# A layer on one core: half of the normalized tiles transposed by DMA, the feed-forward weight loaded behind them, and a new schedule string

## The chip, the cores and the metric

The kernel runs on one core of a Trainium2 chip. The core has TensorE (PE in the profile; the loading of its stationary operand is listed as PEld), VectorE (DVE), ScalarE (ACT), GpSimd (POOL) and SyncE (SP), which here only issues DMAs. Matmuls read SBUF and write one of eight banks of PSUM; DVE and ACT read PSUM. The metric is the device time of one execution in microseconds; less is better.

## The reference

One transformer-like layer on 2048 tokens of width 640, in bf16. The input is normalized, and from the normalized input two branches are computed and summed with the input itself:

```python
xn = _layernorm(x)                      # (x - mean) / sqrt(var + 1e-5)
# attention: 32 query heads of 20, one head of K and V for all of them
q = (xn @ wq) -> [32 heads, 2048, 20];  k = xn @ wk;  v = xn @ wv
p = softmax(q k^T * 20 ** -0.5)         # 32 x 2048 x 2048
attn = concat_heads(p @ v) @ wo
# feed-forward, 640 -> 1728 -> 640
ffn = silu(xn @ w1) @ w2
out = x + attn + ffn
```

The large part is the score matrix: 32 heads times 2048 keys times 2048 queries, each exponentiated.

## The kernel before, in words

**Tiling.** The 2048 tokens are 16 tiles of 128. Queries are treated in four quarters of 512 (QC), heads in groups of four (HG), which gives 32 groups (NGR), each with 16 key tiles: 2048 score tiles of 128 keys by 512 queries. Four heads of width 20 lie on four strips of 32 partitions, so four score matmuls can use four row strips of PE at the same time (`s_mm`, recorded at line 1052). The value product of one key tile and four heads is four matmuls into four column strips (`pv_mms`, line 1175), accumulated in the PSUM bank UB, number 7. A further column of V gives the softmax's sum.

**Two ways to exponentiate.** ACT takes score tiles from two or three neighbouring banks and applies Exp in one instruction (line 1140), written to a ring Ebuf. DVE takes batches of four tiles, the four heads of one key tile: `dve_job` adds a bias and stores int16, whose bits read as bf16 are a power of two with a linear mantissa (line 1336). Two shifted copies of it (`dve_advance`, by POOL at line 1375 or by DVE at line 1380) correct the linear mantissa, and all three go through the value product. So a batch by DVE costs three groups of value matmuls, one by ACT costs one. The batch lies in one of the buffers `z_t`: three of their own and two in `zx`, and its copies in `s_t`.

**Prologue.** `pro_fill` orders the beginning in four blocks of four token tiles. `ln_pair` computes statistics on DVE (lines 550, 552, 554; for tiles 5 and 7 on ACT), the reciprocal root on POOL (line 559), and the normalized tile on DVE (first four, line 575) or POOL (line 572), into a ring `xn_ring` of XNR = 5 tiles. `tr_job` transposes a tile by five PE transposes of 128x128 (line 582) into a PSUM bank and copies it to `xnT` by ACT (first two, line 591) or DVE (line 594). Then `kT_job` makes K for four tiles (line 608; copied by ACT at line 618), `v_job` makes V (lines 632 and 640), and blocks 0 and 1 end with a chunk of Q (`q_job`; `QAT`). Q is scaled by DVE (line 679) and moved to the head strips by small DMAs (line 692).

**Feed-forward and output.** `h_job` makes one 128-wide chunk of the hidden layer: five matmul sets, tanh on ACT (line 756), product on DVE (line 759). `out_job` and, for the last quarter, `y_job` and `fin_job` multiply with w2 and wo in halves of 320 columns; `col_mm` (line 434) issues such a matmul as four column strips, `row_mm` (line 441) as row strips that can ride along with score matmuls. The 14th hidden chunk has only 64 real rows; for two quarters at a time it is made together (`h_pair`), rows 0 to 63 for the even quarter, 64 to 127 for the odd one, with zeros in the rest.

**What sets the order.** Nothing is ordered at run time. A planner in `build` runs through the work with assumed durations (`Sched`, `est`, `commit`) and writes down one order for each engine; `emit` adds the semaphore waits. Each engine then does its list in order. When several PE instructions are ready, `step_pe` picks by kind: scores for ACT ("s"), prologue ("m0"), score tiles for DVE ("d"), value products ("p", "pd"), other matmul jobs ("m", "l"). Its thresholds are in BASE, and every 10 us of planned time one letter of the string PLAN chooses a variation from RULES. In the prologue, score runs go alternately to banks 0 to 2 and 3 to 4 (ABUFS), other jobs to banks 5 and 6 (XBANKS), and DVE gets no score tiles (EARLY = 0). SP issues DMAs in order too, by the priority that `dma` is given; a DMA that must wait holds the ones behind it. The weight w1 (line 1435) has no wait before it and is issued between the first DMAs of Q; w2 (line 1438) and wo wait for the Q of group 1.

```python
dma("w1", lambda e: e.dma_start(w1_sb[:, :, :], wrow(B_w1)), D * F * 2, writes=[res("w1")], prio=1.0)
```

Of the kernel before, what the change touches and what calls it, by code (L numbers as in the profile page):

```python
# [37 lines left out]
XBANKS = (5, 6)  # L38
# [7 lines left out]
XNR = 5  # L46
# [35 lines left out]
EARLY = 0  # L82
# [14 lines left out]
BASE = dict(hold2=0, bnd=4, pj=6000.0, rows=0, rowmin=3, lagmax=6, lagp=0, lagj=6, openlag=5, late=-0.02, lead=0.01, leadmax=0.02, need=460.0, hold=300.0, dwant=600.0, slack=550.0, dnow=400.0, hungry=0.0, patience=0.0, keep=460.0, open=2, zcap=9, stay=0.0, homes=1, want=1, claim=6)  # L97
RULES = dict(a={}, b=dict(keep=0.0), c=dict(lagp=3), d=dict(lagp=5), e=dict(lagp=0), f=dict(patience=200.0), g=dict(dwant=0.0),
             h=dict(zcap=4), i=dict(zcap=3), j=dict(homes=0), k=dict(leadmax=-1.0, lead=-1.0), l=dict(lead=0.08, leadmax=0.1),
             m=dict(need=560.0), n=dict(hold=0.0), o=dict(stay=460.0), p=dict(open=1), q=dict(slack=400.0), r=dict(hungry=1000.0), s=dict(claim=9), t=dict(open=3), u=dict(claim=4), v=dict(want=2), w=dict(slack=700.0), x=dict(hold2=4), y=dict(bnd=0), z=dict(pj=-1e9), A=dict(rows=0), B=dict(rows=2, rowmin=2), C=dict(pj=2000.0), D=dict(openlag=3), E=dict(pj=8000.0), F=dict(hold2=3), G=dict(rows=1))  # L100
PLAN = "aaanGtxBBExhEhmxadrBBzraCBBEGqtrztfFzrqhwnpofocotyxddmGjvmpBaBitntqo"
# [17 lines left out]
class Op:  # L119
    __slots__ = ("eng", "fn", "occ", "lat", "pre", "reads", "writes", "prio", "mode", "slots",  # L120
                 "start", "fin", "done", "deps", "inc", "job", "first", "last", "gate", "on_commit", "seq", "name",
                 "dma_sem", "dma_val", "port", "run", "cut", "ends", "sync")

    def __init__(self, eng, fn, occ, lat=0.0, pre=(), reads=(), writes=(), prio=5.0, mode=None, slots=None,
# [24 lines left out]
        self.sync = None  # L149
        self.ends = (True, True)  # L150
# [52 lines left out]
class Sched:  # L203
# [71 lines left out]
    def commit(self, op, start):  # L275
# [20 lines left out]
        elif e == "sp":  # L296
            self.t[e] = start + op.occ
            own = 3300.0 if op.name == "dma wv" else 800.0 if op.name.startswith("dma pk") else 2000.0 if op.name.startswith("dma la") else 0.0
            self.dma_free = max(self.dma_free, start + 1300.0) + (op.lat - 800.0 if op.name.startswith("dma pk") else op.lat)
# [19 lines left out]
def build(nc, A_x, A_wq, A_wk, A_wv, A_wo, B_x, B_w1, B_w2, out, stack):  # L319
# [257 lines left out]

    def tr_job(n):
# [87 lines left out]
    def q_job(qc, k):  # L666
# [11 lines left out]
        xq_read[qc].append(job)  # L678
        op = Op("dve", lambda v: v.tensor_scalar_mul(q_st[:, st, :], bk(job.bank), QSCALE), t_dve(512), 140,  # L679
# [26 lines left out]
    xq_read = {k: [] for k in range(QC)}  # L706
    t_users = {}
    out_done = {}

    def h_pair(qb):  # L710
# [13 lines left out]
        for q in (qa, qb):  # L724
            xq_read[q].append(job.ops[-1])
        ts = (qb * FC + fk) % 2
# [16 lines left out]
    def h_job(qc, fk):  # L743
# [9 lines left out]
        xq_read[qc].append(job)  # L753
        ts = (qc * FC + fk) % 2
# [3 lines left out]
        extra = [norm_op[n] for n in range(NT)] + [o for n in range(NT) for o in tr_ops[n]] if par == 1 else [norm_op[n] for n in range(QTP + 6, QTP + 9)]  # L758
# [107 lines left out]
    def out_job(qc, i, hf):  # L866
        e0, e1 = hf * HALF, (hf + 1) * HALF
        mms = ffn_mms(qc, i, e0, e1, True, False) + o_mms(qc, i, e0, e1, False, True)
        job = pe_job(f"out{qc}_{i}_{hf}", mms, 19 * 140, gate=lambda: (qc, NG - 1) in pack_op, dyn=True)
        sl = (QTP * qc + i) % 3  # L870
# [18 lines left out]
    def y_job(qc, i, hf):  # L889
        e0, e1 = hf * HALF, (hf + 1) * HALF  # L890
        mms = ffn_mms(qc, i, e0, e1, True, not YC[i]) + o_mms(qc, i, e0, e1, False, True, range(YC[i]))
        job = pe_job(f"y{qc}_{i}_{hf}", mms, (14 + YC[i]) * 140, dyn=True)
        op = Op("dve", lambda v: v.scalar_tensor_tensor(out=yx[:, i, e0:e1], in0=bk(job.bank, 0, HALF), scalar=0.5,  # L893
# [114 lines left out]
    att = {"sgroup": 0, "pgroup": 0, "n": 0, "items": 0, "value": 0.0}  # L1008
# [49 lines left out]
    def plan(n):  # L1058

        if pro or n == 0:  # L1060
            buf = ABUFS[n % 2]
# [195 lines left out]

    def z_idle(k):
        b = z_last[k]
# [5 lines left out]
    def claim():  # L1265
        if z_slot() is None:
            return None
        g = att["sgroup"]
# [805 lines left out]
```

## Time and profile before

| | |
|---|---|
| median of three runs | 693.72 us (693.70 to 693.74) |
| profiled execution | 693.9 us |
| its span, first to last instruction | 692.1 us, TensorE clock 1.000 |
| busy PE / DVE / ACT / POOL | 680.5 / 572.0 / 673.5 / 593.0 us |
| score tiles by ACT | 655 instructions, 652.5 us busy |
| score tiles by DVE | 656 instructions, 428.8 us busy |
| moved by DMA | 28.97 MB |

The profile is one execution. Its views give the busy time of each engine over the span or a stretch of it; groups of equal instructions by source line, with their busy time, the mean of one and the idle time before them; the order of time; the chain of work that ended last; and DMA issues with the time until they landed. Lines are those of the kernel before; a helper's line stands for everything that calls it.

### The profile page before, as it was taken

The numbers are of one execution on the slowest core, as the hardware profiler recorded it, in microseconds if no ns is written. First come the engines' busy times: TensorE is split into PE (matmuls) and PEld (weight loads), VectorE is DVE, ScalarE is ACT, GpSimd is POOL, SyncE is SP. The second block draws the span as 40 slices with busy tenths as digits, with TensorE's granted clock in tenths as the row PEclk, the third lists the DMA queues.
The fourth block names the chain that finished last, engine by engine and source line by source line (L and its number), as shares of the span: only waits on it lengthen the run. The fifth ranks groups of instructions, "written<-read, shape, count | busy, mean of one in ns | idle before, by whom it ended". The sixth has DMA issues, their size and how long they took to land.

```text
span 692.1 us, 22655 instructions
## 1 busy us (share of the span) xinstructions
PE 680.5 (98%) x9908; PEld 229.7 (33%) x9911; DVE 572.0 (83%) x977; ACT 673.5 (97%) x727; POOL 593.0 (86%) x355
## 2 busy tenths in 40 slices
PE   8999999999999999999999999999999999999998
PEld 5432222222222333322223333322222333333344
DVE  7788889988988788789989878789898877888843
ACT  6899999999999999999999999999999999999993
POOL 6658999899988789898998879989889999988890
PEclk9999999999999999999999999999999999999999
DMA  8642220222221222233202222122222202232201
GB/s 223 194 158 39 20 22 14 35 33 27 22 19 14 37 39 24 29 74 35 27 9 28 31 29 33 22 63 41 30 20 21 22 19 31 31 68 23 23 7 40
DMA packets 34241, 28.97 MB, mean 42 GB/s; under 512 B 15486, under 2 KB 29662, under 8 KB 34142
## 3 DMA queue, kind: packets, MB, share of 16 engines
q1 hardware_dynamic: 33854, 27.20, 25.5%
q8 instruction: 77, 1.26, 0.7%
q10 hardware_dynamic: 288, 0.33, 0.1%
q14 instruction: 22, 0.18, 0.1%
HBM read 11.09 MB, written 2.62 MB: 20 GB/s over the span
## 4 chain that ended last, share of the span: by engine, by line
ACT 57%; PE 35%; DVE 5%; POOL 3%; issue 1%; DMA 0%
ACT sbt L1140 53%; PE psall L434 11%; PE psall L1175 11%; PE psall L1052 11%; ACT sbt L756 3%; POOL sbt L1375 2%; DVE sbt L1336 1%; DVE sbt L552 1%; DVE sbt L550 1%; DVE sbt L594 1%; POOL sbt L836 0%; DMA sbt<-in_A_x_dram 0%; PE psall L608 0%; PE psall L973 0%; DVE sbt L679 0%
## 5 line engine op out<-in xcount | busy, mean ns | idle before, releaser
L1140 ACT ACTIVATE sbt<-psall 128x1024 bf16<-128x1024 f32 (+1 forms) x655 | 652.5, 1220 | 2.2 <-PE psall L1052 1.7
L1375 POOL TENSOR_SCALAR sbt<-sbt 128x2048 int16<-128x2048 int16 x279 | 530.5, 1901 | 62.7 <-DVE sbt L1380 12.7
L1336 DVE TENSOR_SCALAR sbt<-psall 128x512 int16<-128x512 f32 x656 | 428.8, 684 | 79.6 <-PE psall L1052 72.0
L1052 PE MATMUL psall<-sbt 32*128 32x512 bf16 x2048 | 265.9, 384 | 3.7 <-ACT sbt L1140 1.8
L1175 PE MATMUL psall<-sbt 128*32 128x512 bf16 x3360 | 267.7, 384 | 1.2 <-DVE sbt L1223 0.4
L434 PE MATMUL psall<-sbt 128*32 128x320 bf16 (+2 forms) x3844 | 226.6, 331 | 0.7 <-ACT sbt L1140 0.5
L1052 PEld LDWEIGHTS psall<-sbt 32*128 32x128 bf16 x2048 | 70.0, 91 | 248.8 <-ACT sbt L1140 194.9
L434 PEld LDWEIGHTS psall<-sbt 128*32 128x32 bf16 x3844 | 83.9, 95 | 77.7 <-issue 46.9
L1175 PEld LDWEIGHTS psall<-sbt 128*32 128x32 bf16 x3360 | 66.0, 94 | 115.1 <-issue 82.4
L836 POOL TENSOR_TENSOR sbt<-sbt 128x512 bf16<-128x512 f32 x30 | 38.3, 1276 | 6.8 <-DVE sbt L1380 4.8
L759 DVE SCALAR_TENSOR_TENSOR sbt<-sbt,psall 128x512 bf16<-128x512 bf16 x52 | 35.5, 683 | 5.6 <-ACT sbt L756 4.9
L1380 DVE TENSOR_SCALAR sbt<-sbt 128x2048 int16<-128x2048 int16 x49 | 39.8, 827 | 0.2
L756 ACT ACTIVATE sbt<-psall 128x512 bf16<-128x512 f32 x52 | 39.5, 760 | 0.0
L1223 DVE COPY sbt<-psall 128x512 f32<-128x512 f32 x31 | 21.1, 682 | 2.3 <-PE psall L1175 2.2
L441 PE MATMUL psall<-sbt 32*128 32x320 bf16 (+1 forms) x60 | 20.5, 342 | 0.1
L1648 PE MATMUL psall<-sbt 128*32 128x256 bf16 (+1 forms) x264 | 18.1, 370 | 1.2 <-DVE sbt L474 1.2
L878 DVE SCALAR_TENSOR_TENSOR sbt<-psall,sbt 128x320 bf16<-128x320 f32 x24 | 11.6, 483 | 3.7 <-PE psall L434 2.6
L679 DVE TENSOR_SCALAR sbt<-psall 128x512 bf16<-128x512 f32 x20 | 13.5, 674 | 0.1
L893 DVE SCALAR_TENSOR_TENSOR sbt<-psall,sbt 128x320 f32<-128x320 f32 x8 | 3.9, 485 | 9.8 <-PE psall L434 9.7
L572 POOL TENSOR_SCALAR sbt<-sbt 128x640 bf16<-128x640 bf16 x12 | 10.4, 878 | 1.5 <-DVE sbt L564 1.2
L559 POOL TENSOR_TENSOR sbt<-sbt 128x2 f32<-128x2 f32 x8 | 5.6, 695 | 6.4 <-DVE sbt L557 6.1
L1648 PEld LDWEIGHTS psall<-sbt 128*32 128x32 bf16 x264 | 7.3, 113 | 6.2 <-issue 3.4
(63 smaller groups left out, 111.9 us busy)
## 6 DMA issues: line engine op xcount, KB each, us to landing
sbt<-sbt SPq DMA_DIRECT2D x120, 64.0 KB, 3.8
sbt<-in_A_x_dram SPq DMA_DIRECT2D x28, 160.0 KB, 3.3
sbt<-sbt SPq DMA_DIRECT2D x213, 20.0 KB
out_dram<-sbt SPq DMA_DIRECT2D x14, 160.0 KB, 1.9
sbt<-in_B_w_dram SPq DMA_DIRECT2D x1, 2160.0 KB, 12.7
sbt<-in_B_w_dram SPq DMA_DIRECT2D x1, 2080.0 KB, 8.2
sbt<-sbt SPq DMA_DIRECT2D x75, 8.0 KB
sbt<-in_A_wq_dram SPq DMA_DIRECT2D x1, 800.0 KB, 6.8
```

The costliest lines, as they stand in the source:

```text
L434: ins = pe.matmul(ps[j * SLOT:(j + 1) * SLOT, b * BANK + off:b * BANK + off + n], w[:, j * SLOT:(j + 1) * SLOT], x, start=start, stop=stop ...
L756: t = Op("act", lambda a: a.activation(t_buf[0:rows, ts, :], bk(job.bank, 0, QW, rows=rows), AF.Tanh, scale=0.5), t_act(512), 215, pre=[jo ...
L759: u = Op("dve", lambda v: v.scalar_tensor_tensor(out=hT[par][0:rows, fk, :], in0=t_buf[0:rows, ts, :], scalar=1.0, in1=bk(job.bank, 0, QW, ...
L836: nm = pool(lambda e: e.tensor_tensor(oU[:, us, :], U_sb[:, us, :], Rrep, ALU.mult), 1356.0, pre=[uc] + lc + pack_op.get(divmod(g - 2, NG) ...
L1052: return pe.matmul(bk(b), kT_rep[i * SLOT:(i + 1) * SLOT, kt * P:(kt + 1) * P], qT[i * SLOT:(i + 1) * SLOT, g % NQ, :], start=True, stop=T ...
L1140: return a.activation(Ebuf[:, es * QW:es * QW + w], ps[:, buf[0] * BANK:buf[0] * BANK + w], AF.Exp, scale=ESCALE)
L1175: ins = pe.matmul(ps[i * SLOT:(i + 1) * SLOT, UB * BANK:UB * BANK + QW], lhsT, rhs, start=(first and k < HG), stop=(last and k >= len(lst) ...
L1223: uc = Op("dve", lambda v: v.tensor_copy(U_sb[:, us, :], bk(UB)), t_dve(512), 140, pre=[pv] + up, reads=[sc.banks[UB]], writes=[res("U", u ...
L1336: p1 = Op("dve", lambda v: v.tensor_scalar(z16[:, i * QW:(i + 1) * QW], bk(job.bank), ZBIAS, 0.0, ALU.add, ALU.max), t_dve(QW) + 2.0, 140, ...
L1375: op = pool(lambda v, t=t, j=j, zin=zin: v.tensor_scalar(t.bitcast(I16), zin, float(SHIFT[j]), 1.0, ALU.add, ALU.mult), POOL_SHIFT, 0.0, p ...
L1380: op = dve(lambda v, t=t, j=j, zin=zin: v.tensor_scalar_add(t.bitcast(I16), zin, float(SHIFT[j])), t_dve(N, 4), prio=SPRIO - 0.01 * j, **args)
L1648: ins = pe.matmul(ps[i * SLOT:(i + 1) * SLOT, UB * BANK:UB * BANK + n], zero_t[:, 0:SLOT], zero_t[:, 0:n], start=fresh, stop=fresh, tile_p ...
```

## The change: what it does

- Tiles 8 to 15 (TRD = 8) are transposed by `tr_dma`: one transposing DMA from SP per tile, from `xn_ring` to `xnT`, with the highest priority on SP. The five PE transposes, the PSUM bank and the DVE copy go. The planner assumes 150 bytes per ns and 1300 ns more for it.
- `xn_ring` has eight tiles. All hidden chunks now wait for the whole prologue's normalization and transposes, since the ring lies partly in their buffer.
- w1 is issued only when the transposes of tiles 8 to 15 have landed.
- In the prologue, score runs are two banks each, on 0 and 1 or 2 and 3 (ARUN), and bank 4 is added to the other jobs' banks.
- DVE may take score tiles in the prologue (EARLY = 1) once tile 7 is normalized and the Q of group 1 is there; it then claims from the group behind ACT's.
- Three more batch buffers come from wq and w1 after their last reader (`Z_LENT`).
- The last hidden chunk is multiplied as the next to last, and in output jobs it may be issued as row strips, only the two that hold its 64 rows (`short`, `half`).
- The first jobs of the last quarter (`y_job`) may be made earlier.
- BASE has a pause before the next score run while ACT still has more than 520 ns of work (`stay`), two new thresholds (`pace`, `lagl`), and RULES and PLAN are new in part.

```diff
-XBANKS = (5, 6)
+XBANKS = (4, 5, 6)
+ARUN = ((0, 1), (2, 3))
-XNR = 5
+XNR = 8
+TRD = 8
+WTR = 4
+T_TR = 1300.0
+TR_RATE = 150.0
-EARLY = 0
+EARLY = 1
+EARLYN = 7
+EARLYG = 1
-BASE = dict(hold2=0, bnd=4, ..., zcap=9, stay=0.0, ...)
+BASE = dict(pace=-1.0, lagl=3, half=6, hold2=0, bnd=4, ..., zcap=9, stay=520.0, ...)
-PLAN = "aaanGtxBBExhEhmxadrBBzraCBBEGqtrztfFzrqhwnpofocotyxddmGjvmpBaBitntqo"
+PLAN = "aabgyzrzpFaxBGBrmJtxvEfyhdBwBrmxJaaawwdBhBKfiwkxkaaGxzGBmooBBtdttgtr"
...
+    NZ1 = len(z_t)
+    z_t.append(wq_sb[:, :, :].rearrange("p c d -> p (c d)")[:, 0:HG * QW])
+    z_t += [w1f[:, QTP * D + 2 * P + k * HG * QW:QTP * D + 2 * P + (k + 1) * HG * QW] for k in range(2)]
...
-    xn_ring = [h1f[:, (6 + i) * D:(7 + i) * D] for i in range(XNR)]
+    xn_ring = [h1f[:, (6 + i) * D:(7 + i) * D] for i in range(5)] + [h0f[:, (3 + i) * D:(4 + i) * D] for i in range(XNR - 5)]
...
+    def tr_dma(n):
+        xnT_op[n] = dma(f"tr{n}", lambda e: e.dma_start_transpose(xnT[:, :, n * P:(n + 1) * P], xn_ring[n % XNR]), P * D * 2,
+                        reads=[res("xn", n % XNR)], writes=[res("xnT", n)], pre=[norm_op[n]], prio=-1.0)
+        tr_ops[n] = [xnT_op[n]]
...
+    def short(job, qc):
+
+        for op in job.ops:
+            if hc_op[(qc, FC - 1)] in op.pre and op.cut is not None:
+                op.rows = tuple(range(HG))[:HG // 2] if qc % 2 == 0 else tuple(range(HG))[HG // 2:]
+        return job
...
-        for fk in range(FC):
+        for fk in [*range(FC - 2), FC - 1, FC - 2]:
...
-            buf = ABUFS[n % 2]
+            buf = ARUN[n % 2]
...
-        g = att["sgroup"]
+        g = att["sgroup"] + (1 if pro and EARLYG else 0)
...
             for n in range(4 * kc, 4 * kc + 4):
+                if n >= TRD:
+                    tr_dma(n)
+                    continue
                 j = tr_job(n)
...
+        d_w["w1"].pre += [tr_ops[n][0] for n in range(max(TRD, WTR), NT)]
...
-        if not pro or EARLY and 1 in q_op and all(o.done for o in q_op[1]) and len(xbanks()) >= EARLY:
+        if not pro or EARLY and (EARLYN not in norm_op or norm_op[EARLYN].done) and 1 in q_op and all(o.done for o in q_op[1]) and len(xbanks()) >= EARLY:
...
-        if not job.dyn or not ru.rows or sc.pe_mode != "s" or ...
+        if not job.dyn or not (ru.rows or ru.half) or sc.pe_mode != "s" or ...
+        if pick is None and not job.rest and len(piece.mms) > ru.half > 0:
+            x = next((x for x in list(piece.mms)[1:-1] if len(x.rows) < HG and all(p.done for p in x.pre)), None)
+            if x is not None:
+                pick = next(((x, r) for r in x.rows if r not in busy), None)
```

More of the change, by code (lines that the diff above doesn't have):

```diff
@@ L149, in __init__ @@
         self.sync = None
+        self.rows = tuple(range(HG))
         self.ends = (True, True)
@@ L1256, in build @@
     z_last = [None] * len(z_t)
+    lent_z = {}
+    Z_LENT = {NZ1: ("q", QC * DC), NZ1 + 1: ("h", QC * FC), NZ1 + 2: ("h", QC * FC)}
     def z_idle(k):
+        if k in Z_LENT and k not in lent_z:
+            w, n = Z_LENT[k]
+            if len(w_read[w]) < n or not all(o.done for o in w_read[w]):
+                return False
+            lent_z[k] = sc.order["pe"][-1]
         b = z_last[k]
@@ L1852, in commit_pe @@
                 cur_job[0].mms.remove(x)
-                job.rest[x] = list(range(HG))
+                job.rest[x] = list(x.rows)
             job.rest[x].remove(r)
```

31 lines of the change are left out of this document (19 added, 12 removed).

## The prediction

> **What bounds the kernel now.** I read the head of the page first, then the shares of the chain of waits, the busy time by stretches, the costliest groups with their shapes kept apart, the order of time around the edit, and the DMA issues.
>
> The head of the page and the chain's shares by engine:
>
> ```profile
> span 692.1 us, 22655 instructions
> PE 680.5 (98%) x9908; PEld 229.7 (33%) x9911; DVE 572.0 (83%) x977; ACT 673.5 (97%) x727; POOL 593.0 (86%) x355
> ...
> ACT 57%; PE 35%; DVE 5%; POOL 3%; issue 1%; DMA 0%
> ```
>
> Two engines are full at once, and the chain passes between them. Busy time by stretches (columns: stretch, its length, busy us and count of PE, PEld, DVE, ACT, POOL, then clock, DMA share, GB/s):
>
> ```profile
> 0.00:10.00 10.00, 8.26 (x157) 6.02 (x158) 6.39 (x21) 5.11 (x8) 7.00 (x22) 1.00 0.74 189
> 10.00:20.00 10.00, 9.44 (x135) 5.06 (x134) 9.64 (x35) 9.38 (x12) 6.31 (x8) 1.00 0.92 231
> 20.00:30.00 10.00, 9.59 (x128) 4.56 (x128) 8.72 (x33) 8.26 (x9) 7.27 (x10) 1.00 0.63 226
> 30.00:40.00 10.00, 9.66 (x121) 3.88 (x117) 5.11 (x12) 9.83 (x10) 1.52 (x3) 1.00 0.84 285
> 40.00:50.00 10.00, 9.87 (x133) 2.87 (x129) 9.14 (x15) 10.00 (x13) 7.65 (x5) 1.00 0.20 57
> ...
> 200.00:300.00 100.00, 99.14 (x1505) 32.52 (x1493) 81.75 (x134) 100.00 (x104) 86.56 (x49) 1.00 0.26 36
> ...
> 680.00:693.00 13.00, 8.79 (x238) 6.30 (x228) 5.14 (x10) 1.56 (x3) 0.00 (x0) 0.95 0.15 52
> ```
>
> From 40 us on ACT never rests, so a later gain can come only by taking exponentials away from ACT. The prologue loses 4.9 + 0.6 + 1.7 + 0.2 us of ACT in its first four stretches, and the tail 11.4 us. The change touches the second to fourth stretch and, through the rules, everything behind them; the first stretch and the tail stay.
>
> The groups of the shared work (last part: busy us, mean ns of one, idle before):
>
> ```profile
> L1375 POOL TENSOR_SCALAR sbt<-sbt 128x2048 int16<-128x2048 int16 x279 | 530.5, 1901 | 62.7 <-DVE sbt L1380 12.7 <-DVE sbt L1336 9.7 <-PE psall L1175 8.0
> L1336 DVE TENSOR_SCALAR sbt<-psall 128x512 int16<-128x512 f32 x656 | 428.8, 684 | 79.6 <-PE psall L1052 72.0 <-PE psall L441 3.0
> ...
> L1140 ACT ACTIVATE sbt<-psall 128x1024 bf16<-128x1024 f32 x573 | 555.0, 1172 | 0.3
> L1140 ACT ACTIVATE sbt<-psall 128x1536 bf16<-128x1536 f32 x82 | 124.6, 1555 | 1.9 <-PE psall L1052 1.7
> ```
>
> A score tile is 128x512. ACT exponentiates 573 x 2 + 82 x 3 = 1392 of them, DVE 656, together 2048. The page has both ACT forms together at 652.5 us:
>
> ```profile
> L1140 ACT ACTIVATE sbt<-psall 128x1024 bf16<-128x1024 f32 (+1 forms) x655 | 652.5, 1220 | 2.2 <-PE psall L1052 1.7
> ```
>
> So a tile costs ACT 652.5 / 1392 = 0.469 us, and a batch of four that DVE takes over saves ACT 1.88 us. What it costs PE is read from the order of time on PE:
>
> ```profile
> 60.81 0.39 PE L1052 MATMUL psall<-sbt 32*128 32x512 bf16 x4
> 61.13 0.62 PE L434 MATMUL psall<-sbt 128*32 128x512 bf16 x8
> 61.68 0.39 PE L1052 MATMUL psall<-sbt 32*128 32x512 bf16 x2
> 62.00 1.06 PE L1175 MATMUL psall<-sbt 128*32 128x512 bf16 x16
> 62.99 0.39 PE L1052 MATMUL psall<-sbt 32*128 32x512 bf16 x4
> 63.32 0.40 PE L1175 MATMUL psall<-sbt 128*32 128x512 bf16 x4
> ```
>
> A score set holds PE 0.32 us (60.81 to 61.13) whether two or four tiles ride in it. Two value groups of four matmuls hold it 0.55 us, four hold it 0.99, so one more is 0.22. A batch by DVE needs three value groups where ACT's needs one: +0.44 us of PE.
>
> **The change part by part.** *Eight tiles leave PE and DVE.* Between 21 and 37 us stand exactly the groups that go:
>
> ```profile
> L594 DVE COPY sbt<-psall 128x640 bf16<-128x640 bf16 x8 | 3.7, 485 | 1.4 <-PE psall L582 1.4
> ...
> L582 PE MATMUL psall<-sbt 128*128 128x128 bf16 x40 | 3.6, 221 | 0.0
> ```
>
> This removes 3.6 us of PE and 3.7 us of DVE, and eight uses of a PSUM bank. Bounds for PE: 0, if its time is filled by waits, and 3.6; I take 3.6, since PE was busy over nine tenths there.
>
> The Trainium skill ("TensorE: Matmul & The Clock Gate", Part 4: PE-mode transpose) gives about 275 ns for one 128x128 transpose inside a kernel, which as an estimate would make 40 of them 11 us. The trace disagrees: 40 take 3.6 us here, because they are pipelined, and the sum goes by that.
>
> *Eight DMAs come onto SP's queue.* Order of time around them (start, length, engine, line):
>
> ```profile
> 16.30 1.41 SPq L1435 DMA_DIRECT2D sbt<-in_B_w_dram  x1
> ...
> 24.39 5.11 SPq L692 DMA_DIRECT2D sbt<-sbt  x7
> ...
> 29.25 1.74 POOL L572 TENSOR_SCALAR sbt<-sbt 128x640 bf16<-128x640 bf16 x2 [0.30 <-DVE sbt L564]
> ...
> 30.73 0.39 SPq L1438 DMA_DIRECT2D sbt<-in_B_w_dram  x1
> ...
> 32.22 0.89 DVE L594 COPY sbt<-psall 128x640 bf16<-128x640 bf16 x2 [0.68 <-PE psall L582]
> ...
> 35.88 0.64 ACT L618 ACTIVATE sbt<-psall 128x512 bf16<-128x512 f32 x1
> ...
> 37.14 2.05 DVE L1336 TENSOR_SCALAR sbt<-psall 128x512 int16<-128x512 f32 x3 [0.61 <-PE psall L1052]
> ...
> 49.33 0.73 ACT L756 ACTIVATE sbt<-psall 128x512 bf16<-128x512 f32 x1
> ```
>
> Now the last two tiles are normalized by 30.99 and transposed by 33.11, 2.1 us later; K for tiles 12 to 15 is copied at 35.88, about when ACT has used up the first twelve. No row shows a transposing DMA. The nearest are these (KB each, us from issue to landing):
>
> ```profile
> sbt<-sbt SPq DMA_DIRECT2D x120, 64.0 KB, 3.8
> sbt<-in_A_x_dram SPq DMA_DIRECT2D x28, 160.0 KB, 3.3
> ...
> sbt<-in_B_w_dram SPq DMA_DIRECT2D x1, 2160.0 KB, 12.7
> sbt<-in_B_w_dram SPq DMA_DIRECT2D x1, 2080.0 KB, 8.2
> ```
>
> Bounds: 3.3 us, the load of as many bytes, and 9.5 us, the 64 KB row's rate on 160 KB. I take 3.8: a move within SBUF. The planner allows 4.4 (1.3 + 163,840 / 150 = 1.1, + 0.7 + 1.3), so nothing ordered behind them should stall. The last tile is then 1.7 us later behind its normalization (3.8 against 2.1). Against that, the four copies of tiles 8 to 11 no longer stand before the last statistics on DVE, 4 x 0.485 = 1.9 us, and eight buffers in place of five let POOL run ahead. Taken at nothing; if the cover fails it costs those 1.7 us of ACT once. SP's own issuing: seven pieces of Q took 5.1 us, 0.73 each; eight more are 5.8 us in a stretch from 17.75 to 33 where SP was not full. What waits in that queue is the second half of those Q pieces, and group 1 behind them: 2 to 3 us later, but no longer behind the 2160 KB weight.
>
> *The weight goes behind them.* From issue at 16.30 to some 35; it lands between 43 and 48, by the two weight rows. Its first use shows at 49.33. Cover: 1 to 6 us. With the second weight issued ahead of it, 8.2 us more, it would be late by up to 7; then feed-forward jobs slip behind attention work that is ready, and nothing is lost but order. Nothing taken; bound +2.
>
> *Score runs of two and two banks in the prologue, a third spare bank.* Between 12.8 and 37 us ACT ran 18 exponentials, alternately three and two tiles, 45 tiles in 20.9 us, which is 0.464 a tile:
>
> ```profile
> L1140 ACT ACTIVATE sbt<-psall 128x1536 bf16<-128x1536 f32 (+1 forms) x18 | 20.9, 1249 | 1.5 <-PE psall L1052 1.5
> ```
>
> The whole span's mean, nearly all two-tile, is 0.469: 45 x 0.005 = 0.2 us. Taken +0.2.
>
> *DVE starts on scores before the prologue ends.* It now begins at 37.14. It needs group 1's Q pieces (24.39 + 5.11 = 29.50, and 30.73 landed), so it can start near 31: some six us, eight tiles, two batches. This is where the shift below finds room on DVE. More than five batches can't be ahead (five buffers until a weight is done with), and 13 tiles are done by 48 us already (DVE's score tiles alone, by stretches):
>
> ```profile
> 37.00:48.00 11.00, 8.48 (x13) 1.00 0.45 154
> ```
>
> *Short last feed-forward chunk.* 32 output jobs have a chunk with only 64 real rows; two row groups of it may ride in score sets. One 320-wide chunk holds PE 0.66 / 4 = 0.165 us with its share of the switch:
>
> ```profile
> 654.97 0.73 PE L434 MATMUL psall<-sbt 128*32 128x320 bf16 x16
> 655.63 0.82 PE L1052 MATMUL psall<-sbt 32*128 32x512 bf16 x4
> ```
>
> All would save 32 x 0.14 (without the switch) = 4.4 us, none 0. Sets of four leave no row free, sets of two leave two; I take half, 2.2 us.
>
> *The rest* (later buffers in used-up weights, the order of chunks, earlier last-quarter jobs, the pause before scores, the string): order only. It could win or lose; a switch saved is 0.32 - 0.22 = 0.1 us, so a tenth of 655 score runs is 6.5 us either way. Taken at nothing.
>
> *The sum.* PE has 3.6 + 2.2 = 5.8 us to spare, ACT none. Moving x batches to DVE brings them level: 5.8 - 0.44 x = 1.88 x, x = 2.5, and both end 4.7 us sooner. DVE and POOL have the room: 2.5 batches are 10 tiles of 428.8 / 656 = 0.65, or 6.5 us of DVE, and five shifts of 1.9, against 79.6 and 62.7 us of waiting and the 3.7 removed. Half of the ACT gaps between 20 and 30 us go too, 0.9, as the transposes and bank uses between score runs go. Less 0.2: together -5.4. The profiled execution took 693.9 us (692.1 and 1.8 around it), so 688.5 for it; against the median of 693.72, 0.2 lower, 688.3.
>
> **The rivals.** *The transposes land late (slower).* Order is fixed when the program is built; each us beyond the allowed 4.4 delays K for tiles 12 to 15, and ACT takes key tiles in order, so it idles. For it: 9.5 us by the slowest row. Landing at 9.5 costs 5.1 and with the gain kept ends level; if, besides, they pass one at a time at 2.5 us a tile, the eighth is 8 x 2.5 = 20 us after the first at about 20, at 40 and not 35, and with the 9.5 us at its end it is some 10 us late: 688.3 + 10 = 698. It decides from 5.4 us late. Against it: loads of the same size land in 3.3.
>
> The Trainium skill ("VectorE: DVE Perf Modes", The three transpose paths) speaks for it: 1309 ns for a 128x128 block by DMA, and TensorE preferred. As an estimate, five blocks a tile one after another are 6.5 us, and eight tiles 52 us. The same skill ("DMA: Bandwidth & Descriptors", Latency and other measured facts) gives 261 GB/s for transposing DMAs, which is an estimate of 0.63 us a tile and no delay. No run here shows either yet.
>
> *The new order starves ACT (slower).* A pause before scores that is too long leaves ACT without tiles: 1% of the 640 us at 100% is 6.4 us, 694.7 with the gain kept. Against it: PE's waits for ACT are many and ACT's for PE few.
>
> *The freed time is not taken up (no change).* PE fills it with waits, ACT keeps 1392 tiles: only the gap time, 0.9 less 0.2: 693.0.
>
> *More than balance (faster).* All short chunks ride along (4.4) and a tenth of the switches is saved (half of 6.5): PE has 3.6 + 4.4 + 3.2 = 11.2 spare, x = 4.8, -9.1 and the gaps: 684.
>
> **How the numbers follow.** Forecast 0.47 (its own range 686 to 691.5), more than balance 0.22, not taken up 0.11, order starving ACT 0.10, late transposes 0.10. Predicted 688.3. Within 0.2% (1.4 us, about what a measurement of this kernel tells from no change) lie most of "not taken up" and a little of the slower two: 0.09; faster 0.73; slower 0.18. For 8 in 10: 683 leaves out part of the fast case, 696 the worst of the late one.
>
> **What would show it.** Right: no PE transposes and DVE copies after about 21 us; DMA transposes landing in 3 to 5 us; the first DVE score tile near 31; ACT over 9.5 in 20 to 30; DVE tiles up from 656 to about 666. Wrong: K's matmuls for tiles 8 to 15 waiting for a DMA, an ACT gap of microseconds at 30 to 40, or ACT below 99% after 50. The prediction falls if DVE's count stays while ACT's gaps stay.

## The result, and the profile after

The changed kernel takes 706.64 us (median of four, 705.34 to 707.81) against 693.71 us (693.62 to 693.74) for the kernel before, measured beside it. The ratio is 1.0182 with a 95% interval of 1.0169 to 1.0195: slower by 12.9 us, where 5.4 us less were forecast. The profiled execution took 705.34 us, 1.3 below the median.

The head of the page and the chain's shares by engine, of the changed kernel:

```profile
span 703.4 us, 22552 instructions
PE 683.2 (97%) x9846; PEld 226.8 (32%) x9849; DVE 569.1 (81%) x962; ACT 673.9 (96%) x733; POOL 605.0 (86%) x362
...
ACT 77%; PE 16%; DVE 3%; DMA 1%; SPq 1%; POOL 1%; issue 0%; POOLq 0%
```

ACT has as much work as before, 673.9 us against 673.5, in a span that is 11.3 us longer: it waits more. The groups of the shared work say that the split is the old one:

```profile
L1169 ACT ACTIVATE sbt<-psall 128x1024 bf16<-128x1024 f32 (+1 forms) x661 | 654.2, 1243 | 7.3 <-PE psall L1081 7.2
...
L1373 DVE TENSOR_SCALAR sbt<-psall 128x512 int16<-128x512 f32 x656 | 432.4, 686 | 96.5 <-PE psall L1081 89.8 <-PE psall L452 3.0
```

DVE has 656 score tiles in both kernels: no batch moved. Busy time by stretches (columns as in the prediction) shows where ACT waits:

```profile
10.00:20.00 10.00, 9.20 (x126) 4.95 (x124) 9.82 (x35) 8.81 (x14) 5.64 (x8) 1.00 0.87 234
20.00:30.00 10.00, 9.84 (x125) 3.34 (x125) 7.40 (x27) 9.43 (x11) 8.67 (x11) 1.00 0.53 81
30.00:40.00 10.00, 6.21 (x72) 2.09 (x71) 0.54 (x3) 6.31 (x7) 0.73 (x2) 0.79 0.34 70
40.00:50.00 10.00, 9.69 (x105) 2.85 (x109) 5.76 (x12) 6.49 (x7) 1.46 (x1) 0.70 0.89 311
50.00:60.00 10.00, 9.63 (x96) 2.33 (x93) 8.21 (x14) 8.93 (x11) 8.33 (x6) 0.83 0.68 249
60.00:100.00 40.00, 38.86 (x500) 11.58 (x492) 35.70 (x59) 39.76 (x47) 32.94 (x19) 1.00 0.24 29
200.00:300.00 100.00, 99.19 (x1535) 33.78 (x1536) 79.70 (x127) 100.00 (x106) 93.77 (x52) 1.00 0.26 34
...
690.00:704.00 14.00, 10.12 (x280) 7.46 (x272) 5.61 (x11) 0.00 (x0) 0.00 (x0) 1.00 0.14 49
```

Between 30 and 60 us ACT misses (is idle for) 3.7 + 3.5 + 1.1 = 8.3 us, where it missed 0.2 before. Later it is full again, and behind its last exponential PE still has 10 us of matmuls. The order of time on SP, and then the instructions on PE and DVE that waited (the bracket is the idle time before them and who ended it):

```profile
20.79 6.01 SPq L590 DMA_TRANSPOSE sbt<-sbt  x4
26.85 1.53 SPq L709 DMA_DIRECT2D sbt<-sbt  x2
28.43 2.53 SPq L590 DMA_TRANSPOSE sbt<-sbt  x2
31.00 1.49 SPq L709 DMA_DIRECT2D sbt<-sbt  x2
32.54 2.53 SPq L590 DMA_TRANSPOSE sbt<-sbt  x2
35.11 2.11 SPq L709 DMA_DIRECT2D sbt<-sbt  x3
40.28 0.41 SPq L1478 DMA_DIRECT2D sbt<-in_B_w_dram  x1
...
36.92 1.06 PE L624 MATMUL psall<-sbt 128*128 128x512 bf16 x2 [2.07 <-DMA sbt<-sbt]
40.31 0.60 PE L1081 MATMUL psall<-sbt 32*128 32x512 bf16 x2 [1.78 <-DMA sbt<-sbt]
...
40.95 1.29 DVE L1373 TENSOR_SCALAR sbt<-psall 128x512 int16<-128x512 f32 x2 [9.52 <-PE psall L1081]
```

The answer for the transposing DMAs alone:

```profile
L590 SPq DMA_TRANSPOSE sbt<-sbt x8: 1200/1268/1832, 20.8 to 33.8; - x8
...
DMA to landing us min/median/max: 2.6/2.7/3.7
```

They land in 2.7 us, sooner than the 3.8 forecast. But each holds SP's queue for 1.27 us (median), not the 0.73 of a piece of Q: the eight take 6.01 + 2.53 + 2.53 = 11.1 us of it, of which some 0.3 us are a wait for GpSimd, and the last piece of group 1's Q leaves at 37.2 us, against 29.5 before. From 20.8 to 37.2 us SP has no other pause. Two instructions on PE wait for what this queue issues. The K matmuls for tiles 12 to 15 wait 2.07 us for the last transposes. In the middle of the same K job the order has a score set of group 1 for DVE, which waits for all of Q's pieces until 40.31; some 1.8 us of that are a late landing of the last pieces, which the last section comes back to. PE does its list in order, so ACT's scores behind those two come late: that is the first stall. What SP has queued behind it is late too, down to the moment when GpSimd normalizes group 0, that is, multiplies its value product by the reciprocals of the softmax sums, which come to it by DMAs from SP. First in the changed kernel, then in the kernel before:

```profile
79.47 1.28 POOL L863 TENSOR_TENSOR sbt<-sbt 128x512 bf16<-128x512 f32 x1 [0.79 <-DMA sbt<-sbt]
```

```profile
65.03 1.27 POOL L836 TENSOR_TENSOR sbt<-sbt 128x512 bf16<-128x512 f32 x1 [0.66 <-DVE sbt L1380]
```

### The profile page after: what moved, and what is told of

The parts are those of the page before. It is cut to its first block, busy times and chain, and to the rows that moved or that the text cites. A ratio compares the mean times of both kernels' runs of the same rounds, so it can differ in the third digit from the quotient of the medians.

```text
span 703.4 us, 22552 instructions
## 1 busy us (share of the span) xinstructions
PE 683.2 (97%) x9846; PEld 226.8 (32%) x9849; DVE 569.1 (81%) x962; ACT 673.9 (96%) x733; POOL 605.0 (86%) x362
## 4 chain that ended last, share of the span: by engine, by line
ACT 77%; PE 16%; DVE 3%; DMA 1%; SPq 1%; POOL 1%; issue 0%; POOLq 0%
ACT sbt L1169 73%; PE psall L1204 5%; PE psall L445 5%; PE psall L1081 5%; ACT sbt L776 3%; DMA sbt<-sbt 1%; DVE sbt L561 1%; DVE sbt L563 1%; SPq L590 0%; DMA sbt<-in_A_x_dram 0%; SPq L709 0%; DVE sbt L568 0%; POOL sbt L570 0%; PE psall L1002 0%; POOL sbt L1412 0%; DVE sbt L1373 0%
## 5 line engine op out<-in xcount | busy, mean ns | idle before, releaser
L1412 POOL TENSOR_SCALAR sbt<-sbt 128x2048 int16<-128x2048 int16 x286 | 542.6, 1897 | 60.9 <-DVE sbt L1417 17.2
L1081 PE MATMUL psall<-sbt 32*128 32x512 bf16 x2048 | 269.4, 387 | 8.7 <-ACT sbt L1169 4.8
L445 PE MATMUL psall<-sbt 128*32 128x320 bf16 (+3 forms) x3728 | 227.5, 333 | 1.0 <-ACT sbt L1169 0.4
L1081 PEld LDWEIGHTS psall<-sbt 32*128 32x128 bf16 x2048 | 71.1, 91 | 257.9 <-ACT sbt L1169 190.9
L445 PEld LDWEIGHTS psall<-sbt 128*32 128x32 bf16 (+1 forms) x3728 | 80.1, 96 | 79.1 <-issue 49.7
L1204 PEld LDWEIGHTS psall<-sbt 128*32 128x32 bf16 x3360 | 67.9, 94 | 116.0 <-issue 79.4
L452 PE MATMUL psall<-sbt 32*128 32x320 bf16 (+1 forms) x122 | 39.4, 323 | 0.0
L1417 DVE TENSOR_SCALAR sbt<-sbt 128x2048 int16<-128x2048 int16 x42 | 35.7, 864 | 0.1
L1689 PE MATMUL psall<-sbt 128*32 128x256 bf16 (+1 forms) x296 | 20.2, 362 | 1.2 <-DVE sbt L485 1.2
L452 PEld LDWEIGHTS psall<-sbt 32*128 32x128 bf16 x122 | 11.1, 91 | 0.9 <-PE psall L445 0.7
L1689 PEld LDWEIGHTS psall<-sbt 128*32 128x32 bf16 x296 | 8.2, 109 | 7.3 <-issue 4.3
```

The costliest lines, as they stand in the source:

```text
L445: ins = pe.matmul(ps[j * SLOT:(j + 1) * SLOT, b * BANK + off:b * BANK + off + n], w[:, j * SLOT:(j + 1) * SLOT], x, start=start, stop=stop ...
L452: return pe.matmul(ps[0:w.shape[-1], b * BANK:b * BANK + n], w[k], x[k], start=start, stop=stop, tile_position=(r * SLOT, 0))
L1081: return pe.matmul(bk(b), kT_rep[i * SLOT:(i + 1) * SLOT, kt * P:(kt + 1) * P], qT[i * SLOT:(i + 1) * SLOT, g % NQ, :], start=True, stop=T ...
L1204: ins = pe.matmul(ps[i * SLOT:(i + 1) * SLOT, UB * BANK:UB * BANK + QW], lhsT, rhs, start=(first and k < HG), stop=(last and k >= len(lst) ...
L1412: op = pool(lambda v, t=t, j=j, zin=zin: v.tensor_scalar(t.bitcast(I16), zin, float(SHIFT[j]), 1.0, ALU.add, ALU.mult), POOL_SHIFT, 0.0, p ...
L1417: op = dve(lambda v, t=t, j=j, zin=zin: v.tensor_scalar_add(t.bitcast(I16), zin, float(SHIFT[j])), t_dve(N, 4), prio=SPRIO - 0.01 * j, **args)
```

## The experiments

A string of rules belongs to the kernel for which it was chosen: a new plan would change all of the order at once. So in each run below the order was planned as it stands, and one thing was edited in it afterwards. The kernel before took 693.97 or 693.98 us beside the first eight, 694.32 beside the last four. Diffs show what matters; left-out lines are marked.

**Plain copies in the transposes' place.** The transposition itself is left out.

```diff
-        xnT_op[n] = dma(f"tr{n}", lambda e: e.dma_start_transpose(xnT[:, :, n * P:(n + 1) * P], xn_ring[n % XNR]), P * D * 2,
+        xnT_op[n] = dma(f"tr{n}", lambda e: e.dma_start(xnT[:, :, n * P:(n + 1) * P], xn_ring[n % XNR].rearrange("p (c t) -> p c t", c=DC)), P * D * 2,
```

> The order of the changed kernel on every engine, with the eight transposing DMAs replaced by plain copies of the same 160 KB into the same place (so xnT holds untransposed tiles 8 to 15: the transposing is left out). A plain issue held SyncE 0.73 us where a transposing one held it 1.27. Theory A, the issue time on SyncE's queue is what delays the last Q pieces and K for tiles 12 to 15: 8 x 0.54 = 4.3 us less in front of them, the last Q piece lands near 35 instead of 40.3, ACT's idle time between 30 and 60 us falls from 8.3 us to 2 or less, the clock stays at 1.00, and the time is 697 to 699 us. Rival B, the waiting is for the data and not for the queue, or the loss is in the new order behind 60 us: 704 to 707 as now.

Measured: 702.0 us, ratio 1.0121 (1.0097 to 1.0145). Only 4.6 us came back, where 7.6 to 9.6 were expected. The first stall is gone, by this kernel's stretches, but a later one stands in its place:

```profile
30.00:40.00 10.00, 9.60 (x137) 3.58 (x135) 3.23 (x10) 9.16 (x11) 0.62 (x2) 1.00 0.58 177
40.00:60.00 20.00, 19.64 (x237) 5.52 (x233) 19.22 (x32) 20.00 (x23) 15.25 (x9) 1.00 0.61 219
60.00:80.00 20.00, 16.96 (x199) 4.96 (x198) 15.18 (x26) 17.23 (x20) 14.77 (x9) 0.96 0.31 32
```

```profile
73.78 1.26 POOL L863 TENSOR_TENSOR sbt<-sbt 128x512 bf16<-128x512 f32 x1 [3.42 <-DMA sbt<-sbt]
```

ACT misses 2.8 us between 60 and 80. GpSimd waits 3.42 us for group 0's sums, whose DMAs stand in SP's queue behind the loads of wo, of its end, of w2 and 22 pieces of Q; the shift for DVE's next batch stands behind it on GpSimd. So there are two stalls in a row, and taking away the first uncovers the second.

**Plain copies that hold the queue as long as the transposes.** Nothing is transposed here either. A small DMA is issued ahead of each copy.

```diff
+    spare = sb([P, 8 * SLOT], BF16)
+    spare_sem = sem("d_spare")
...
-        xnT_op[n] = dma(f"tr{n}", lambda e: e.dma_start_transpose(xnT[:, :, n * P:(n + 1) * P], xn_ring[n % XNR]), P * D * 2,
+        def two_issues(e):
+            e.dma_start(spare[:, (n - TRD) * SLOT:(n - TRD + 1) * SLOT], zero_t[:, 0:SLOT]).then_inc(spare_sem, 16)
+            return e.dma_start(xnT[:, :, n * P:(n + 1) * P], xn_ring[n % XNR].rearrange("p (c t) -> p c t", c=DC))
+        xnT_op[n] = dma(f"tr{n}", two_issues, P * D * 2,
```

> As the run with plain copies (the transposing is left out), but each copy has a second small DMA issued ahead of it that nobody waits for, so that each tile holds SyncE for about 2 x 0.7 = 1.4 us with plain DMAs only. Theory A (SyncE's issue time): the loss is back, 704 to 708 us, with ACT idle 7 to 10 us between 30 and 60. Rival (something proper to the transposing, its landing or its traffic): as the run with plain copies.

Measured: 704.42 us, ratio 1.0145 (1.013 to 1.0161), as expected. Half of what the plain copies had won is lost by issue time alone, with nothing transposed. Between 30 and 60 us ACT misses 4.2 + 1.3 = 5.5 us again (7 to 10 were expected), where it missed 0.8 with the copies alone:

```profile
30.00:40.00 10.00, 6.55 (x74) 2.23 (x74) 0.82 (x4) 5.80 (x7) 0.53 (x1) 0.85 0.33 80
40.00:50.00 10.00, 10.00 (x121) 3.03 (x119) 7.16 (x14) 8.68 (x10) 3.06 (x2) 0.81 1.01 366
```

The last piece of Q leaves later here than in the changed kernel, at 37.8 us, but SP's next load, which waits for it, goes on at 39.0 and not at 40.3. The 2.2 us by which this run is faster are near that difference in landing; that it is the reason is not shown.

**Group 1's score sets wait for their own pieces of Q.**

```diff
-            o = dma(f"q{st}", lambda e, r0=r0, r1=r1, d0=d0, slot=slot: e.dma_start(
+            o = dma(f"q{st}" + ("g" if qc == 0 and k == 1 and idx == 1 else ""), lambda e, r0=r0, r1=r1, d0=d0, slot=slot: e.dma_start(
...
+    later = {o for g in (2, 3) for o, _ in part[g]}
+    theirs = {r for g in (2, 3) for _, r in part[g]}
+    for op in sc.order["pe"]:
+        if op.mode == "s" and op.deps & later and not theirs & set(op.reads):
+            op.deps -= later
```

> The changed kernel in its own order; group 1's score matmuls wait only for the two Q pieces that they read (with a semaphore of their own), not for the five pieces of groups 2 and 3 behind the last transposes. Theory A2, the wait to 40.3 us for the last piece is part of the loss: the 2.3 us wait on PE goes, the wait for the last transposes to 36.5 us stays; 2 to 4 us faster than the changed kernel, 701 to 704. If only K's wait counts: 705 to 707.

Measured: 707.23 us, ratio 1.0191 (1.0175 to 1.0207). A miss: no gain. The first stall shrinks from 8.3 to 3.7 us, but then GpSimd waits 5.45 us at its normalization (79.06 us), and ACT misses 6.5 us between 60 and 100.

**TensorE kept busy through its two waits**, with seven and nine sets of zero matmuls into a bank that they leave as it is.

```diff
...
+    pe_list = sc.order["pe"]
+    for name, count in (("kT12", 7), ("sd1_11_0", 9)):
+        at = next(i for i, o in enumerate(pe_list) if o.name == name)
+        for _ in range(count):
+            w = Op("pe", zeros_mm, 216.0, mode="p", name="warm")
+            w.deps = {zero_op}
+            pe_list.insert(at, w)
```

> The changed kernel with 7 matmul sets of zeros in front of K for tiles 12 to 15 and 9 in front of the first DVE score tile, where PE waits for DMAs (they add zero to the open accumulation). Theory C, the stall also costs by the clock, which was granted at 0.50 from 36 to 46 us and 0.56 to 0.59 from 56 to 60: with the clock at 1.00 the 14 us at half speed give back 3 to 6 us: 700 to 703. Rival: those matmuls weren't what the chain waited for, no more than 1 us: 704.5 to 707.

Measured: 706.8 us, ratio 1.0185 (1.0164 to 1.0206). A miss too. The clock is 1.00 in the whole stretch, and the time is the same:

```profile
30.00:60.00 30.00, 27.61 (x365) 9.07 (x363) 17.11 (x33) 24.04 (x28) 12.48 (x9) 1.00 0.63 210
```

ACT still misses 6.0 us here and 3.2 later, between 80 and 100 us. So the clock is not what remains of the first stall. What it is worth is not shown: the later stall can have hidden a gain, and K for tiles 12 to 15 starts at 38.4 us here and not at 36.9, because the last transposes, issued at the same time, landed 1.6 us later.

**The loads of wo, its end and w2 moved behind group 0's sums on SP.**

```diff
+    sp = sc.order["sp"]
+    moved = [o for o in sp if o.name in ("dma wo", "dma wo_end", "dma w2")]
+    rest = [o for o in sp if o not in moved]
+    at = [i for i, o in enumerate(rest) if o.name == "dma lc0"][HG - 1] + 1
+    sp[:] = rest[:at] + moved + rest[at:]
```

> The changed kernel's order, with eleven DMAs moved back on SyncE's queue alone: wo, the eight small wo_end and the two remainders of w2 are issued behind the softmax-sum DMAs of group 0 (they held SyncE 2.3, 6.0 and about 2.8 us). Theory S, the first 80 us are set by SyncE's queue, and the time follows from when POOL can normalize group 0 (it began at 79.5 us in the changed kernel, 65.0 before; in all kernels with the changed order so far the span ends 624 to 626 us behind it): that moves to 70 to 73 us and the time to 698 to 702 us. The first stall, 30 to 45 us, is ahead of the moved DMAs and stays (ACT idle about 8 us in 30 to 60). Rival, the queue behind 40 us doesn't count: 705 to 708.

Measured: 709.93 us, ratio 1.0223 (1.0198 to 1.0249): a miss, slower still. The moved loads now stand ahead of group 1's sums, and the second one of w2 must wait for the first. SP's order of time, and DVE's waits between 56 and 110 us:

```profile
76.23 0.55 SPq L1481 DMA_DIRECT2D sbt<-in_B_w_dram  x1
81.03 0.50 SPq L1483 DMA_DIRECT2D sbt<-in_B_w_dram  x1
81.58 0.63 SPq L851 DMA_DIRECT2D sbt<-sbt  x1
```

```profile
DVE sbt L854 <- DMA sbt<-sbt: 4.7, 1, 4.7
```

SP stands still from 76.8 to 81.0, so DVE's reciprocal waits 4.7 us with all of DVE's score tiles behind it. The place was badly chosen: the same stall, one group later.

**That move with the own pieces of Q, and with the plain copies.**

> Both: the eleven DMAs moved back, and group 1's scores waiting only for their own two Q pieces. Alone, the second gained nothing, because the queue then stalled PE at 73 to 80 us by as much as it had saved. Theory S: with the queue relieved, it now gains its 4 us: ACT idle 30 to 60 about 4 us, none behind it, 696 to 699 us. If it gains nothing again: as the run with only the DMAs moved.

> Plain copies in place of the transposing DMAs (the transposing is left out), and the eleven DMAs moved back. Theory S: both stalls gone, ACT idle under 2 us from 30 to 100 us, normalization of group 0 below 68 us, and 696 to 698 us is what the new order is worth by itself, with a tail 3 us longer than before; so still slower than before. Rival, DMA transposes are all that is wrong with the change: 688 to 694.

Measured: 704.86 us, ratio 1.0157 (1.0138 to 1.0177), and 702.28 us, ratio 1.0121 (1.0102 to 1.014): both misses. The same reciprocal waits 4.1 and 4.0 us in them, so neither is free of the later stall.

**The kernel before with the load on SP alone.** Its order, its PE transposes and all its computation are kept; eight transposing DMAs of a resident weight into unused space are issued where tiles 8 to 15 are normalized, and nobody reads them. The hidden chunks of the first quarter, which use that space later, are made to wait for them; no such wait shows in the trace.

```diff
+    sp = sc.order["sp"]
+    spare = h0f[:, 3 * D:3 * D + 4736]
+    for n in range(8, NT):
...
+        w = Op("sp", lambda e, n=n: e.dma_start_transpose(spare[:, (n - 8) * D:min((n - 7) * D, 4736)].rearrange("p (c t) -> p c t", t=P), wq_sb[:, 0, 0:min(D, 4736 - (n - 8) * D)]), 700.0, name="dma " + key)
...
+        w.deps = {norm_op[n], d_wq}
+        at = next(i for i, o in enumerate(sp) if o.start > norm_op[n].fin)
+        sp.insert(at, w)
+        for fk in range(FC):
+            hc_op[(0, fk)].deps.add(w)
```

> The kernel before, in its own order, with its PE transposes; beside them eight transposing DMAs of a resident weight into unused space (seven as large as a tile, one of two blocks), on SyncE's queue where tiles 8 to 15 have been normalized. Nothing waits for what they write. Theory S: about 9.5 us of issue time on SyncE, of which its waits in that stretch (4.0, 1.3, 1.0 and about 2 us) hide half or more; the Q pieces and group 0's sums come 3 to 6 us later, ACT idles 2 to 5 us more, 695 to 699 us. Rival, the queue has slack enough: 693.5 to 694.5.

Measured: 700.51 us, ratio 1.0096 (1.0074 to 1.0117): 6.5 us lost, more than expected, with no wait for any transposed data and no new order. The stretches of this kernel:

```profile
30.00:40.00 10.00, 6.47 (x77) 2.82 (x73) 2.34 (x8) 8.29 (x8) 1.62 (x3) 1.00 0.62 82
40.00:60.00 20.00, 18.93 (x210) 4.96 (x210) 15.20 (x24) 15.07 (x17) 10.87 (x6) 0.83 0.58 183
```

ACT misses 6.6 us here, and a score set on PE waits 4.25 us, until 40.94, for a piece of Q that left SP at 39.7. The size is not that of the changed kernel: w1 is still issued ahead here, one of these DMAs held SP for 2.41 us in the median and not 1.27, and the first four for 9.46 us and not 6.01.

**The loads moved far back**, where SP idles: wo and w2 behind group 2's sums, wo's end at 215 us of the plan. Their first uses are planned at 209 and 686 us.

```diff
+    sp = sc.order["sp"]
+    early = [o for o in sp if o.name in ("dma wo", "dma w2")]
+    last = [o for o in sp if o.name == "dma wo_end"]
+    sp[:] = [o for o in sp if o not in early + last]
+    at = [i for i, o in enumerate(sp) if o.name == "dma lc0"][2 * HG - 1] + 1
+    sp[at:at] = early
+    at = next(i for i, o in enumerate(sp) if o.start > 215000)
+    sp[at:at] = last
```

> Changed kernel, same order on TensorE, ScalarE, VectorE and GpSimd; on SyncE's queue the load of wo and the pair that completes w2 stand behind group 2's sums (planned 98 us, needed at 209) and the eight pieces of wo's end at 215 us (needed at 686). Theory (SyncE's queue is what runs late): group 0's normalization on GpSimd, at 79.5 us in the changed kernel, comes at 66 to 70, and nothing waits for group 1's sums at 80 to 100 as when the same transfers were put there. The first stall (ScalarE idle 30 to 60 us, 8.3 us) is ahead of the move and stays: 703 to 706. Rival (the first stall alone sets the end, the later lateness is hidden by it): no gain at all, 706 to 707. Rival (these loads are not what holds the queue): normalization stays near 77 to 79.

Measured: 703.36 us, ratio 1.0129 (1.0114 to 1.0144), within the theory's range. The place of the normalization was a miss, 77.26 us and not 66 to 70: it starts without any wait, because GpSimd itself is late by the first stall. From 50 to 680 us ACT is full.

**Moved far back, and own pieces of Q.**

> The run before this one, and in addition group 1's score sets wait for their own two Q pieces only. Theory (both stalls come from SyncE's queue, and only with both shortened does time come back): ScalarE idle 30 to 60 us falls from 8.3 to about 3.7 and in 60 to 100 stays under 1: 700 to 702. Rival (the half-speed clock or another wait takes the place): over 704.

Measured: 700.14 us, ratio 1.0085 (1.0067 to 1.0103), as expected. With the later stall gone, the shorter first wait is worth 3.2 us, where alone it had been worth nothing. This is the fastest of the runs that keep the DMA transposes and compute the whole layer, and still slower than the kernel before.

**Moved far back, and plain copies.**

> Plain copies in place of the transposing DMAs (the transposition is left out), and wo, w2's pair and wo's end moved back as in the first of these runs. Theory: neither stall is left; what remains against the kernel before is the new order's own worth with its longer tail: 697 to 699, ScalarE idle in 30 to 100 under 2 us. Rival (the new order is as good as the old one once the queue is not late): 692 to 695. Rival (the loss is in the order itself, not in the queue): 701 or more, as with the plain copies alone (702.0).

Measured: 697.0 us, ratio 1.0038 (1.0023 to 1.0053). Neither stall is left. In these last three runs GpSimd's normalization of group 0 and the time move together: 77.26, 73.62 and 70.50 us; 703.36, 700.14 and 697.0 us. There, one more us of lateness at the start costs about one us at the end.

What remains, 2.7 us, goes with the new order. Stretches of the kernel before, then of this one:

```profile
300.00:600.00 300.00, 297.93 (x4288) 95.69 (x4289) 255.51 (x416) 299.53 (x324) 271.69 (x150) 1.00 0.24 29
...
680.00:696.00 16.00, 8.79 (x238) 6.30 (x228) 5.14 (x10) 1.56 (x3) 0.00 (x0) 0.93 0.12 42
```

```profile
300.00:600.00 300.00, 294.73 (x4212) 92.07 (x4204) 253.08 (x409) 300.00 (x325) 272.99 (x152) 1.00 0.24 29
...
680.00:696.00 16.00, 12.11 (x332) 8.78 (x324) 5.61 (x11) 1.12 (x3) 0.76 (x1) 1.00 0.13 44
```

ACT is full and ends as early as before. But PE is busy 3.2 us less in the middle, and has 3.3 us more to do after 680 us, when ACT is done. By the waits of PE between 40 and 680 us, it waits for ACT's banks 4.9 us here, 1.8 before:

```profile
PE psall L1081 <- ACT sbt L1169: 4.9, 14, 0.6
```

```profile
PE psall L1052 <- ACT sbt L1140: 1.8, 7, 0.5
```

**Moved far back, own pieces, and TensorE kept busy**, by the same sets of zero matmuls.

> The second of these runs, and zero matmuls where TensorE waits, at kT12 and at the first VectorE score tile of group 1, so that its granted clock stays at 1.00. The transposes are kept. Theory: with the queue relieved the clock's half speed is next in line: 0.5 to 2 us below the run without them, 698 to 701. Rival (clock without weight for the end, as before): no difference, or up to 1 us slower by the zero matmuls' own time.

Measured: 703.88 us, ratio 1.0132 (1.0116 to 1.0149): 3.7 us slower than without the zero matmuls, a miss for both theories. The second place had no wait left to fill, and the zeros held PE for 3.75 us (recorded under the helper's line), with ACT's next scores behind them:

```profile
39.34 3.75 PE L1975 MATMUL psall<-sbt 128*32 128x512 bf16 x36
...
43.46 1.29 DVE L1373 TENSOR_SCALAR sbt<-psall 128x512 int16<-128x512 f32 x2 [11.89 <-PE psall L1081]
```

So this run says nothing of the clock. It shows again what a few us on PE cost at this place.

**The account.** Differences of the ratios, at 694 us, split the 1.82% in three steps. Moving the loads far back is worth 0.53% or 3.7 us: loads that stand on SP ahead of group 0's sums and are late once the queue is late. Plain copies besides are worth 0.91% or 6.3 us: the longer issue of the transposing DMAs and what waits for them. The new order keeps 0.38% or 2.6 us. Waiting for the own pieces of Q is not a fourth part: it is worth 0.44% or 3.1 us with the transposing DMAs kept, and is another way to some of the same 0.91%, since the copy run keeps the wait for all pieces. The first two are uncertain by some 1.5 us and the last by 1, since each ratio is by 0.15%; the split also goes by the sequence of the edits, because each stall hides part of the next. How much of the 0.91% is issue, how much the late landing of the last pieces and how much the clock, no run separates. The parts of the new order (short chunk, two-bank runs, pause before scores, string) were not taken apart: that wants a new plan for each.

## Why the prediction was wrong

- **Which step failed: the DMAs on SP.** "SP's own issuing: seven pieces of Q took 5.1 us, 0.73 each; eight more are 5.8 us in a stretch from 17.75 to 33 where SP was not full" took one price for two kinds of DMA. Measured: 1.27 us for one, 11.1 us for the eight. And "2 to 3 us later", taken at nothing, was 7.7 us for the last piece of Q (37.2 against 29.5), and SP's next load, which waits for it, went on 9.6 us later (40.28 against 30.73). The slack counted on in that queue wasn't there: I looked for waits behind the landing of a tile, and not for what else stands in that queue. The run with copies that hold the queue as long, and the kernel before under the load alone, show issue time as a cause without any transposition for the layer.
- **Landing** was right and better: 2.7 us against 3.8. The planner's 4.4 from issue to landing covers it; what its plan had not foreseen is 1.27 us in the queue, for which it has 0.7. ("Landing" counts from the start of the issue, so the 1.27 are part of the 2.7.)
- **The early start of DVE** was wrong by the same cause: 40.95 us and not near 31, later even than the 37.14 of before. The early score set, thought of as room, is itself the second of the two waits. The gap time came in part: ACT is busy 9.43 us between 20 and 30, against 8.26, but 8.81 between 10 and 20, against 9.38.
- **Eight tiles off PE and DVE, and the short chunk**: DVE fell by 572.0 - 568.4 = 3.6 us in the run moved far back with plain copies, as forecast (3.7). PE fell from 680.5 to 678.5 there: 2.0 of the 5.8 us that I had put down for the transposes and the short chunk. The short chunk did ride along, more often than the half that I took: of the matmuls of 320 columns, column strips fell from 2288 to 2172 and row strips rose from 32 to 94, which makes 27 of the 32 short chunks (an estimate: two strips for a short chunk, four for a full one, as many chunks in all). So the sum's "5.8 us to spare" was too large besides; why, these runs don't show. What PE did save came back in part as waits for ACT's banks, 4.9 us against 1.8. (One row of 0.55 us that the prediction reads as two value groups is of line 434, other matmuls of the same shape; nothing hangs on it.)
- **The sum** turned spare PE time into moved batches. None moved: 656 tiles in both, the sign named beforehand under which the prediction falls. The split is written down with the order when the program is built, and a PE that is ahead at run time cannot hand ACT's tiles to DVE. Without the stalls, 697.0 is nearest to the rival "not taken up" (693.0), plus PE work left for the end.
- **Rules and string** at nothing: together with the rest of the new order +2.6 us, inside the 6.5 either way.
- **The weight behind them**: issued at 40.98 and not near 35, it landed in 13.0 us, at 54.0, past the 49.33 of its old first use; the first tanh of the hidden layer now comes at 65.17. No wait for it shows in the changed kernel's waits after 41 us. Whether the later feed-forward costs anything was not tested.
- **The rival that came nearest** was "the transposes land late": K for tiles 12 to 15 waits for a DMA and ACT idles. Its place was right and its price, 698, too low; its mechanism was not, since they land early and hold the queue long.

On the two figures of the Trainium skill in the prediction: an estimate of 6.5 us a tile from 1309 ns a block ("VectorE: DVE Perf Modes", The three transpose paths) was more than twice the 2.7 us measured, and 0.63 us by 261 GB/s ("DMA: Bandwidth & Descriptors", Latency and other measured facts) a quarter of it. Neither speaks of the queue's time. The same page says (Issuing engines are not separate DMA queues) that spreading DMAs over engines saves only the time to initiate one, "which is usually small relative to the DMA itself". Here it is 1.27 of 2.7 us, which is not small.

## What to carry to other kernels

When work moves to DMA, write down the issuing queue as an engine with its own occupancy, price each kind of DMA by itself, among the transfers that run beside it, and follow every later entry of that queue to whoever waits for it; landing time alone says little. Where the order is fixed at build time, time freed on one engine is worth nothing until the plan gives it to the engine that bounds, and an early piece of work placed ahead of its data is a wait for everybody behind it. After taking a stall away, look for the next one before judging: the own pieces of Q gave nothing alone and 3.2 us once the later stall was gone.

## What the runs showed of the hardware

- A transposing DMA of one 128x640 bf16 tile within SBUF held SP for 1.27 us and landed in 2.7 (medians); a plain copy of the same tile held it 0.66 us and landed in 2.6. The time on SP is not fixed: in the kernel before under the load, with w1 issued ahead, it was 1.21 to 3.16 us, and landing took 5.5 us in the median. Why was not tested.
- TensorE's granted clock in the changed kernel was half from 35.8 to 46.0 us, that is, from within the wait of 2.07 us on. With zero matmuls ahead of both waits, where 1.77 us of the first one were left, it stayed at 1.00. By the Trainium skill ("TensorE: Matmul & The Clock Gate", Why this matters for your kernels) gaps of more than about 3 us are the ones to avoid; here the half clock came with one of 2.07, and in the run moved far back with own pieces with a single one of 2.31 (0.50 from 38 to 40 us). In the changed kernel it was also 0.56 and 0.59 in the stretches 56 to 58 and 58 to 60 us, with no such wait ahead; why isn't shown. The first stretch:

```profile
35.80:46.00 10.20, 7.29 (x58) 2.16 (x59) 2.52 (x6) 4.48 (x5) 0.52 (x1) 0.50 0.49 151
```

- The last piece of Q was issued by 37.2 us in the changed kernel, yet its waiters went on at 40.3. SP's next load waits for it, 2.8 us there and 1.0 with plain copies:

```profile
SPq L1478 <- DMA sbt<-sbt: 2.8, 1, 2.8
```

```profile
SPq L1478 <- DMA sbt<-sbt: 1.0, 1, 1.0
```

Between 37.2 and 40.4 the DMA queues of the changed kernel held almost nothing but this:

```profile
DMA packets 63, 0.05 MB, mean 17 GB/s; under 512 B 26, under 2 KB 62, under 8 KB 62
...
q1 hardware_dynamic: 62, 0.04, 4.7%
q8 instruction: 1, 0.02, 2.4%
```

One packet on the instruction queue takes 2.4% of 16 engines' 3.2 us, 1.2 us of one engine. A piece of Q is complete only when all its packets are, so a fetch of instructions ahead of one of them is the likely reason. No run tests it, but the other traces agree. In all six runs with transposing DMAs in the changed kernel's order and without zero matmuls, such a packet starts 0.5 to 0.7 us after the last piece of Q was issued, and SP waits 2.5 to 2.9 us. In the two with zero matmuls it starts near 36 us, just before the last transposes should land; these land late instead, and SP waits 1.0 for Q. In the four with copies it comes when the pieces have landed or nearly so, and SP waits 1.0.
